# Mamba-2 scan and low-rank mixer on one core: V loaded in four transfers, begun behind B and C of the second pair

## The chip, the cores and the metric

The kernel runs on one NeuronCore of one Trainium2 chip. The time is device microseconds (us) of one execution of the program; smaller is better. Several runs of the kernel before are given, and one further execution was recorded by the hardware profiler.

## The reference: a chunked scan, then a mixer

The inputs are x (4 batches, 8 heads, 768 steps, 32 wide), a decay a per step, and B and C (16 wide). The scan, cut to what matters:

```python
for c in range(nc):                       # chunks of 32 steps
    cum = np.cumsum(la, axis=-1)          # la = log of the clipped decays
    L = np.exp(cum[:, :, :, None] - cum[:, :, None, :]) * causal
    M = (Cc @ Bc.T) * L
    y[:, :, sl] = M @ xc + (Cc @ state) * np.exp(cum)[..., None]
    state = decay_full * state + sum_j(Bc[j] xc[j] * decay_from_j[j])
```

Its output, with the heads joined to 256 channels, goes through the mixer:

```python
h = xt @ U @ V                            # over the 768 steps, rank 32
u = x + h.transpose(0, 2, 1)
out = u + np.maximum(u @ w_ch1, 0.0) @ w_ch2
```

U (768 x 32), V (32 x 768) and both weights w_ch1 (256 x 1024) and w_ch2 (1024 x 256) are handed over in double precision.

## The kernel before

**Tiling.** A batch's 768 steps are six blocks of 128, one step per partition. Two blocks make a pair, and the twelve pairs (three a batch) are numbered through. B and C of a pair lie in a tile `bc`, x in a tile `x`.

**Loads.** All loads are issued by SyncE (SP), by `begin` (L195 and L196). The B of one pair is two transfers, one a block, with C of the pair issued between them (`load_bc`, L200); x is two transfers (`load_x`, L213). The doubles arrive as pairs of 32-bit words in tiles called `words`. U and V share one of these: `load_v` (L254) fills its second half, `load_u` (L258) its first. V is 32 rows of 768 doubles, cut into four pieces of 192 columns; piece q goes to the partitions from 32q to 32q + 31, so that a partition gets 384 words, or 1536 bytes. Before, one transfer does this: its source pattern has the piece q outermost (4), then 32 rows, then 384 words; its destination has 128 partitions.

**Order.** The order of work is written out by hand. `PLANS[0]` (L35) lists the first loads, which SP issues in that order behind the load of a (L182): B0 is B and C of pair 0, X0 its x, U0 and V0 are U and V. `PLANS[1]` to `PLANS[4]` list the steps of the other engines and the later loads; `follow` (L974) reads them. Lags are counted in pairs against the batch, so that in `PLANS[1]` the index -3 is pair 0 and -2 is pair 1.

**The first steps.** `F5` and `F4` put idle products on TensorE (PE) ahead of the next step. `A0` and `A1` (`decays`, L357) make the decay factors F of all pairs from a, by PE and ScalarE (ACT). `Q` (`prep`, L461) multiplies a part of B or C with F on VectorE (DVE) into the tile `BC`; Q-3.2, Q-3.1 and Q-3.0 are C and the two B of pair 0. `V-3.0.0` and `V-3.1.1` (`turn`, L511; these words have nothing to do with the matrix V) transpose them on PE into T and Cm. `Q-2.0` is B of pair 1, block 0; it stands on DVE ahead of the Cm of V-3.1.1. `K0` (`keep`, L376) makes the factors FD and `kept` by five groups of products on PE, then by `own` and `kept` on DVE (L394 to L397). Q-2.2 and Q-2.1 are C and the other B of pair 1.

`c0` is the first conversion step of U and V together (`to_fp32`, L401): two operations on DVE (L415, L417) and one on ACT (L419), which wait for both. Then come `D` (B times FD into `bd`, L473, on GpSimd in the first batch), `g` (products of T and Cm), `m` and `M` (masks on DVE), `s` and `u` (states), and `n`, `i` and `j` (products into y). `v0` (`spread`, L927) and the mixer use the finished V about twenty microseconds later.

DVE and GpSimd operations of one engine run in program order; DVE's operations all carry line 170, where a helper records them.

Of the kernel before, what the change touches and what calls it, by code (L numbers as in the profile page):

```python
# [32 lines left out]

PLANS = {
    0: (  # L35
        'V0 B0 X0 B1 U0 X1 B2 X2 B3 '),
    1: (
        'F5 A0 A1 Q-3.2 Q-3.1 Q-3.0 F4 V-3.0.0 Q-2.0 V-3.1.1 K0 Q-2.2 Q-2.1 c0 D-3 g-3 D-2 s-3 '
        'V-2.0.2 m-3 u-3 F2 V-2.1.2 M-3 E-1.1 Q-1.0 n-3 c0 g-2 i-3 Q-1.2 E-1.0 Q-1.1 w0 m-2 s-2 '
# [37 lines left out]
def kernel(  # L77
# [31 lines left out]
    NC = S // P  # L109
    NPR = NC // 2  # L110
    DM = NH * D
    RK = moe_U.shape[1]
# [7 lines left out]
    Q = 32  # L120
# [38 lines left out]
    class Kept:  # L159
# [6 lines left out]
        def __getattr__(self, name):  # L166
# [16 lines left out]
        out=a_sb,  # L183
        in_=a.rearrange("(g b) h (c s) -> g (b h c) s", g=2, s=P).rearrange(
            "g r s -> r g s"))
# [4 lines left out]
    def hold(load, until):  # L190

        tc.add_manual_dep(load.ins, until.ins.name, mybir.DependencyInfo(
            mybir.DependencyClass.Sync, mybir.DependencyReason.DATA))

    def begin(**kwargs):  # L195
        op = nc.sync.dma_start(**kwargs)  # L196
        if until:
            hold(op, until.pop())
# [24 lines left out]
    UV = const.tile([P, 2, NC * RK], FP32)  # L223
# [9 lines left out]
    def words_of(dst):  # L233
        p, i, j = dst.shape
        t = raw.tile([P, 2 * WCOLS], INT32, tag="words", name="words", bufs=NWORDS)
        weights.append((dst, t[:p, :2 * i * j]))
        return t[:p, :2 * i * j]
# [10 lines left out]
    U2, V2, w12, w22 = (w.bitcast(INT32) for w in (moe_U, moe_V, moe_w_ch1, moe_w_ch2))  # L248
# [3 lines left out]
    own = {}  # L252

    def load_v():  # L254
        own["UV"] = words_of(UV)
        begin(out=own["UV"][:, 2 * NC * RK:], in_=V2.rearrange("r (q j) -> q r j", q=4))

    def load_u():  # L258
        begin(out=own["UV"][:, :2 * NC * RK].rearrange("p (c r) -> p c r", c=NC),
# [24 lines left out]
    for word in PLANS[0].split():  # L284
        dict(loads, V=lambda n: load_v(), U=lambda n: load_u())[word[0]](int(word[1:]))
# [42 lines left out]
    for g in range(2):  # L328
# [3 lines left out]
        out=la.rearrange("p b c h -> p b h c"),  # L332
# [128 lines left out]
    def prep(k, c=0, n=2):  # L461

        b, q = pairs[k]
        if "BC" not in st.setdefault(k, {}):
            st[k]["BC"] = att.tile([P, 2, 2, NH, N], FP32, tag="BC", name="BC")
        for g in [slice(4) if n == 2 else slice(c, c + 1) if c < 2 else slice(2, 4)]:
            part = st[k]["BC"].rearrange("p i c h n -> p (i c) h n")[:, g]
            vector.tensor_tensor(
                out=part, in0=bc_sb[k].rearrange("p h i c n -> p (i c) h n")[:, g],
                in1=F[:, b, q].rearrange("p h i c -> p (i c) h")[:, g, :, None].to_broadcast(  # L470
                    part.shape), op=ALU.mult)
# [490 lines left out]
    def ytokens_of(k, v):  # L962
# [4 lines left out]
                 j=crossed, y=yout, t=ytokens, L=load, Q=lambda k, c: prep(k, c, 1),  # L967
# [59 lines left out]
```

## Time and profile before

| | |
|---|---|
| Runs of the kernel before | 227.67, 228.96 and 229.0 us, median 228.96 |
| Profiled execution, whole | 229.59 us |
| Its span, first to last instruction | 227.0 us |
| Mean granted TensorE clock | 0.985 |
| Busy: PE, PEld | 218.4 us (96%), 182.2 us (80%) |
| Busy: DVE, ACT, GpSimd | 158.1, 120.9, 6.4 us |
| Chain that ended last | PE 90%, DVE 4%, SP's queue 3%, DMA 1% |
| The load of V | issued at 1.26 us, 192 KB |
| The load of U | issued at 9.32 us, 192 KB, 3.1 us from issue to landing |

The profile divides the span into 40 slices and gives busy tenths of each engine:

```profile
PE   7779999999999999999999999999999999999994
PEclk9995999999999999999999999999999999999999
DMA  3997868990970021662005300200000010010011
```

PE is busy throughout but for the first slices of 5.7 us each. `PEclk` is the clock that PE was granted. The chain of waits is read from the end of the kernel back to its start: every step is the work, the issue or the transfer that released the next one.

### The profile page before, as it was taken

The page shows a single profiled execution, that of the slowest core. Times are in us where ns is not written, and L with a number is a line of the kernel's source. Part 1 is how long each engine was busy: PE and PEld are TensorE (multiplying, and loading weights), DVE is VectorE, ACT ScalarE, POOL GpSimd, SP SyncE. Part 2 cuts the span into 40 slices and gives each one's busy share as a digit, 9 for nine tenths or more (in the row PEclk, how much of TensorE's full clock was granted, in tenths as well). Part 3 has the DMA queues.
Part 4 walks back from the last instruction along what each step waited for, and adds up shares of the span by engine and source line. Part 5 has one row for each costly group of instructions (what it writes and reads, how often), then busy time and mean ns, then how long its engine had stood idle before and what let it go on. Part 6 is the DMA issues. An engine that isn't in the chain of part 4 may idle for free.

```text
span 227.0 us, 6988 instructions
## 1 busy us (share of the span) xinstructions
PE 218.4 (96%) x3016; PEld 182.2 (80%) x3016; DVE 158.1 (70%) x339; ACT 120.9 (53%) x283; POOL 6.4 (3%) x22
## 2 busy tenths in 40 slices
PE   7779999999999999999999999999999999999994
PEld 5648866665675768868998998799998799999994
DVE  3396999897998685879628827878566925765641
ACT  2263565778885334944635715386355524834820
POOL 4032000000000000000000000000000000000000
PEclk9995999999999999999999999999999999999999
DMA  3997868990970021662005300200000010010011
GB/s 79 138 126 119 99 166 222 230 220 8 184 98 1 3 72 15 86 86 72 4 0 75 90 2 3 75 0 0 4 0 3 23 49 0 1 69 3 0 69 69
DMA packets 69234, 14.56 MB, mean 64 GB/s; under 512 B 63508, under 2 KB 67412, under 8 KB 69204
## 3 DMA queue, kind: packets, MB, share of 16 engines
q1 hardware_dynamic: 69204, 14.13, 31.7%
q8 instruction: 23, 0.38, 0.7%
q14 instruction: 7, 0.06, 0.1%
HBM read 10.98 MB, written 3.15 MB: 62 GB/s over the span
## 4 chain that ended last, share of the span: by engine, by line
PE 90%; DVE 4%; SPq 3%; DMA 1%; issue 1%; DVEq 0%
PE x L773 33%; PE z L773 31%; PE y L677 4%; PE y L653 4%; PE w L727 3%; SPq L196 2%; PE w L900 2%; PE x L527 2%; PE w L698 2%; PE w L562 2%; PE w L495 2%; PE x L738 1%; DMA bc<-in_B_dram 1%; PE z L527 1%; DVE BC L170 1%; PE z L738 1%
## 5 line engine op out<-in xcount | busy, mean ns | idle before, releaser
L170 DVE SCALAR_TENSOR_TENSOR words<-words 128x768 fp32r<-128x768 f32 (+6 forms) x44 | 34.6, 804 | 2.1 <-ACT words L419 1.1
L773 PE MATMUL z<-u,w 128*128 128x384 f32 x144 | 32.9, 349 | 0.0
L773 PE MATMUL x<-u,w 128*128 128x384 f32 x144 | 32.6, 346 | 0.0
L778 ACT ACTIVATE x<-x 128x384 f32<-128x384 f32 (+1 forms) x31 | 14.6, 470 | 28.0 <-PE x L773 27.4
L773 PEld LDWEIGHTS z<-u,w 128*128 128x128 f32 x144 | 24.9, 188 | 1.4 <-ACT z L778 0.2
L773 PEld LDWEIGHTS x<-u,w 128*128 128x128 f32 x144 | 24.9, 188 | 1.0
L773 PE MATMUL x<-words,w 128*128 128x384 f32 x120 | 24.7, 340 | 0.2 <-DVE yT L170 0.2
L773 PE MATMUL z<-words,w 128*128 128x384 f32 x120 | 24.6, 336 | 0.0
L778 ACT ACTIVATE z<-z 128x384 f32<-128x384 f32 (+1 forms) x30 | 14.2, 473 | 14.7 <-PE z L773 14.3
L170 DVE SCALAR_TENSOR_TENSOR words<-x,words 128x384 fp32r<-128x384 f32 x24 | 13.3, 553 | 11.7 <-ACT words L807 11.7
L773 PEld LDWEIGHTS x<-words,w 128*128 128x128 f32 x120 | 20.8, 188 | 0.6 <-DVE yT L170 0.4
L773 PEld LDWEIGHTS z<-words,w 128*128 128x128 f32 x120 | 21.1, 188 | 0.0
L170 DVE TENSOR_TENSOR yT<-x,yT 128x384 f32<-128x384 f32 x15 | 8.3, 555 | 16.0 <-PE x L773 15.4
L170 DVE SCALAR_TENSOR_TENSOR words<-z,words 128x384 fp32r<-128x384 f32 x24 | 13.2, 552 | 4.9 <-ACT words L807 4.9
L807 ACT ACTIVATE words<-x 128x384 fp32r<-128x384 f32 x24 | 11.8, 491 | 6.7 <-PE x L773 6.5
L807 ACT ACTIVATE words<-z 128x384 fp32r<-128x384 f32 x24 | 11.8, 491 | 4.5 <-PE z L773 4.5
L170 DVE TENSOR_TENSOR yT<-z,yT 128x384 f32<-128x384 f32 x15 | 8.3, 553 | 8.3 <-PE z L773 8.3
L170 DVE TENSOR_TENSOR BC<-bc,F 128x512 f32<-128x512 f32 (+2 forms) x18 | 9.6, 553 | 4.7 <-ACT F L372 2.5
L170 DVE SCALAR_TENSOR_TENSOR S<-S,kept,w 128x64 f32<-128x64 f32 x40 | 11.2, 280 | 2.2 <-issue 0.5
L653 PEld LDWEIGHTS y<-T,Sm 32*64 32x64 f32 x352 | 9.0, 136 | 4.5 <-issue 1.4
L653 PE MATMUL y<-T,Sm 32*64 32x64 f32 x352 | 12.3, 243 | 0.3 <-DVE settled L170 0.3
L677 PEld LDWEIGHTS y<-M,x 64*32 64x32 f32 x768 | 9.1, 110 | 3.4 <-issue 1.7
(139 smaller groups left out, 387.5 us busy)
## 6 DMA issues: line engine op xcount, KB each, us to landing
words<-in_moe_w_ch_dram SPq DMA_DIRECT2D x7, 512.0 KB, 4.3
x<-in_x_dram SPq DMA_DIRECT2D x24, 128.0 KB, 3.4
out_dram<-o SPq DMA_DIRECT2D x5, 384.0 KB, 2.5
bc<-in_B_dram SPq DMA_DIRECT2D x24, 64.0 KB, 3.3
bc<-in_C_dram SPq DMA_DIRECT2D x12, 128.0 KB, 3.0
out_dram<-words SPq DMA_DIRECT2D x2, 384.0 KB, 4.0
words<-in_moe_w_ch_dram SPq DMA_DIRECT2D x2, 256.0 KB, 3.4
out_dram<-o SPq DMA_DIRECT2D x3, 128.0 KB, 1.7
```

Source lines behind the costliest of these rows:

```text
L170: self.last = call(*args, **kwargs)
L196: op = nc.sync.dma_start(**kwargs)
L495: nc.tensor.transpose(out=tp[:, i, v], in_=s["BC"][:, i, c + v].rearrange("p h n -> p (h n)"), identity=ident)
L527: nc.tensor.matmul(out=g[r][cols, c], lhsT=s["T"][rows, 0, c, cols], rhs=s["Cm"][rows, :, :, ts(2 * c + p, Q)].rearrange("r v t i -> r v i ...
L562: nc.tensor.matmul(out=s["A"][p][ts(r, Q), v], lhsT=s["bd"][half, v, 2 * r:2 * r + 2].rearrange("p h n -> p (h n)"), rhs=x_sb[k][half, v, ...
L653: product = nc.tensor.matmul(out=y[p][ts(r % 2, H), r // 2, c], lhsT=own[ts(r, Q)], rhs=s["T"][ts(r, Q), 1, :, ts(2 * c + p, Q)].rearrange ...
L677: product = nc.tensor.matmul(out=y[p][ts(i, Q), n, c], lhsT=x_sb[k][half, c, h], rhs=s["M"][half, h // 2, c, h % 2], start=fresh(k, p, [i] ...
L698: nc.tensor.transpose(out=t[:, c, g], in_=yT[b][:, g, ts(2 * q + c, P)], identity=ident)
L727: nc.tensor.matmul(out=p[ts(q, Q)], lhsT=U_sb[:, c], rhs=ytok[b][:, c, ts(q // 2, P)], start=(c == 0), stop=(c == NC - 1), skip_group_chec ...
L773: nc.tensor.matmul(out=t, lhsT=lhsT, rhs=rhs, start=start, stop=True, skip_group_check=True)
L778: nc.scalar.activation(t, t, AF.Copy, scale=1.0 + EPS)
L807: nc.scalar.activation(gs[j, m // 2][0][:, m % 2], t, AF.Relu, scale=NEAR)
```

## The change

V is loaded by four transfers, one for each piece, instead of one, each from a plain block of 32 rows and 384 words to 32 partitions. And they are issued behind B and C of pair 1 and ahead of U, instead of first.

```diff
 PLANS = {
     0: (
-        'V0 B0 X0 B1 U0 X1 B2 X2 B3 '),
+        'B0 X0 B1 V0 U0 X1 B2 X2 B3 '),
...
     def load_v():
         own["UV"] = words_of(UV)
-        begin(out=own["UV"][:, 2 * NC * RK:], in_=V2.rearrange("r (q j) -> q r j", q=4))
+        for q in range(4):
+            begin(out=own["UV"][ts(q, Q), 2 * NC * RK:], in_=V2[:, ts(q, 2 * NC * RK)])
```

`ts(q, n)` is the slice from q n to (q + 1) n; Q is 32 and 2 * NC * RK is 384. The place of V's tile among the `words` tiles moves with it, and so does the SP queue: a, B, C, B, x, x (pair 0), B, C, B (pair 1), four parts of V, U, x, x (pair 1), then the loads of pair 2. The order of instructions on PE, DVE, ACT and GpSimd is the same in both kernels.

## Prediction

> **What bounds the kernel now.** I read the engine table first: PE is busy 218.4 of 227.0 us, so whatever PE waits for early on is paid at the end. The slices show that the only weak PE digits stand in the first 15 us, beside a DMA digit that is low (3) in the very first slice. So I went to the chain of waits, in order of time (start, length, who):
> ```profile
> 1.26 0.71 SPq L196
> ...
> 3.13 2.69 SPq L196
> ...
> 7.12 3.19 DMA bc<-in_B_dram
> ...
> 10.33 0.03 DVE BC L170
> ...
> 10.54 0.60 DVE Cm L170 x2
> 11.14 0.44 DVE own L170
> ...
> 11.61 0.52 DVE kept L170
> 12.13 1.32 DVE BC L170 x2
> 13.45 0.54 DVE words L170 x2
> 13.99 0.34 DVE M L170
> ```
> The end of the kernel hangs on SP's issues up to 7.1, then on the landing of one B (pair 1, block 0) at 10.31, then on DVE until 16.2, and from there on PE. The 2.69 us is one DMA issue (the second B of pair 0) where its neighbours take 0.43 to 0.71. The timeline of DVE says what the late B costs:
> ```profile
> 7.36 0.83 DVE L170 TENSOR_TENSOR BC<-bc,F 128x256 f32<-128x256 f32 x3 [2.52 <-ACT F L372]
> 10.33 0.29 DVE L170 TENSOR_TENSOR BC<-bc,F 128x128 f32<-128x128 f32 x1 [2.14 <-DMA bc<-in_B_dram]
> 12.04 1.41 DVE L170 TENSOR_TENSOR BC<-bc,F 128x256 f32<-128x256 f32 x2
> ```
> DVE stands idle 2.14 us for it, and its first BC waited for F, not for data. Stretch by stretch (length, PE, PEld, DVE, ACT, POOL busy, clock, DMA share, GB/s) the transfers are far from full until 7 us:
> ```profile
> 3.00:4.00 1.00, 1.00 (x7) 1.00 (x6) 0.54 (x2) 0.03 (x1) 0.25 (x2) 1.00 0.40 88
> 5.00:6.00 1.00, 1.00 (x6) 1.00 (x6) 0.00 (x0) 0.00 (x0) 0.00 (x0) 1.00 0.51 75
> 7.00:8.00 1.00, 1.00 (x4) 0.54 (x4) 0.64 (x3) 0.33 (x1) 0.00 (x0) 1.00 1.06 154
> ```
> Why: the trace's semaphore records have V's last four increments at 6.14, 6.19, 6.22 and 6.25, where other loads have sixteen, and the 128 packets of V (1536 B, 65 ns each when undisturbed) run from 2.5 to 5.5. B and C of pair 0, issued behind V, land in twelve parts by 5.45 and 6.03 and in four parts at 6.37 to 6.48 and 6.79 to 6.91. So V sits on four DMA engines, the loads behind it wait there, and the fifth issue sticks until V is through (5.82).
>
> **What the Trainium skill says.** "DMA: Bandwidth & Descriptors", "Why a DMA increments its semaphore by 16 and not by 1": a transfer runs on the largest count up to 16 that divides the slowest dimension of both patterns. Before, V has 128 and 4 (q outermost), so four; a transfer of the change has 32 and 32, so sixteen. The four increments agree. The same page, "Rules for kernel authors", advises one 128-partition transfer rather than parts, since parts share the same 16 engines; the trace of before shows a whole that does not have sixteen. "SBUF — State Buffer", "SBUF: two separate sides": a VectorE operation with two SBUF inputs and a GpSimd one lock each other out. Agrees: the two BC beside bd (POOL, 11.93 to 13.30) took 0.78 and 0.71 us, the same shapes elsewhere 0.43 and 0.29. "TensorE: Matmul & The Clock Gate", Part 1: after an idle window of about 3.4 us, free-running, the clock is halved. Agrees: the clock is 0.5 from 16.33 to 23.16, twice 3.41.
>
> **The change, part by part.**
> *V leaves the front.* One issue of 0.71 plus 0.06 goes: B, C and B of pair 0 are issued 0.77 earlier. The sticking issue should take an ordinary 0.58 in place of 2.69. From a's end at 1.20, with 0.43 for the first B and about 0.62 each after it, the B of pair 1 is issued at 4.2 rather than 7.12, 2.9 earlier.
> *What the transfers allow.* Packet records at full flow give 450 B packets (64 B) or 380 x or C packets (128 B) per quarter us, so 0.55 us for a B (1024) and 0.68 for x or C. First B packets came 1.5 after their issue: 2.8 here. B, C, B, x, x, B then is 3 x 0.55 + 3 x 0.68 = 3.7: data through at 6.5, landed about 7.0 against 10.31. Were half of that lost, 8.6. DVE wants it at 8.19 (7.36 + 0.83), so its 2.14 wait goes, or 0.4 of it stays.
> *What is late next.* Not F: the fills on PE hold it at 7.33 as before. After the early BC (8.19 to 8.48) comes Cm, whose transposes end on PE at 8.91: 8.95 to 9.55. Then "own" waits for K0's products, on PE until 10.37 and behind nothing that moves: 10.40 instead of 11.06, a gain of **0.66**. This wait takes the place of the one removed.
> *Behind it.* own 0.52 and kept 0.52 end at 11.44. FD on ACT stood behind T, and T behind Cm: from 11.51 to about 9.9, so bd on POOL starts about 10.2 rather than 11.93 and is through at 11.6. own reads PSUM, kept has one input, so by the page neither should be locked out, and the two BC start at 11.42 with bd nearly done: 0.43 + 0.29 less overlap = 0.65 rather than 1.41, another **0.7**. No row shows own or kept beside POOL; if they were held as BC was, the 0.7 is lost, not more. I take 0.65: **1.3** in all, DVE's words at 12.1 instead of 13.38.
> *Four V issues ahead of U.* Each is 32 rows, 2 packets per engine; the nearest rows are a (0.40) and a weight load of 256 rows (0.37). No row has 32 rows: 0.37 below, 0.79 (the dearest ordinary issue) above; I take 0.42, plus 0.04 between, 1.8 in all. Data cost 128 x 65 ns / 16 = 0.5 us. B of pair 1, block 1, is issued by 6.6 instead of 9.27, so V by 8.4 and U by 9.0 (before 9.90), landing about 10.9 against 12.41. Queued behind V on SP: U, both x of pair 1, the loads of pair 2. x lands near 11.5 and 12.2 (13.31 and 14.32), pair 2's last B near 14 (17.04), wanted about 15.8. No other queue is passed; ACT's and POOL's orders stay. The new waits on five semaphores rather than two ahead of words (DVE at L415, ACT at L419) I put at 0 to 0.2, covered on ACT by its idle time.
> *After 12 us.* DVE's words, M, S, M are back to back until 16.2 and move as one; PE's first product on the second pair's path (y, 16.24) and all after it move by the same 1.3. No wait on a DMA ends a PE stall after 17 us, so nothing there gives it back; the weights' issues wait mostly on DVE and move with it.
> *Sum.* 229.59 of the profiled execution (span 227.0, 2.6 around it) less 1.3 is 228.3. The median is 0.63 lower, 228.96: less 1.3 gives **227.7**.
>
> **The rivals.**
> *The clock is spared too (0.18).* The halved stretch follows the PE gaps at 10.4 to 11.3 and 12.9 to 14.4; the first goes. If the gate then stays open, products of 16.3 to 23.2 shrink: w transposes 0.63 for four at full clock against about 1.05, the others 0.1 to 0.5 a group, some 2.8 together, of which DVE, 70% busy there, lets through 1.5 to 2. Time 227.7 - 1.8 = 225.9. Against: the second gap, set by DVE, stays, and the windows are free-running, so it can fall either way in each run; 227.67 among the runs before may be such a one.
> *The gain is absorbed (0.12).* K0 or bd holds DVE as now, or the gap moves the clock's halving on to dearer products. For it: own moves by 0.66 only, and POOL's overlap is unseen. Time 228.4 to 229.0.
> *U too late: slower (0.08).* The stuck issue is not V's doing and stays, so only 0.77 is won ahead of U, while four V issues at 0.79 cost 3.2: U lands at 12.41 - 0.77 + 3.2 = 14.8. DVE wants it at 12.8 to 13.4; words, and behind it M, S and PE's next products, stand until 14.8, 1.4 later than now: 230.4. It decides from U landing after 13.4. Against: sticking ends as V's data ends, and of the loads behind V only four parts in sixteen are late. Here belongs the case that the parts do not run on sixteen.
>
> **How the numbers follow.** My forecast has 0.62 (own range 227.3 to 228.4 plus run noise, 0.7). The range takes in most of the spared clock below and the absorbed gain above: 225.8 to 229.3. About 1% (2.3 us) is what a measurement can tell from no change, and 1.3 is less. Faster by over 1%: the spared clock and a thin tail of the forecast, 0.22. Slower by over 1% needs 231.3, beyond the late U: 0.04. Within: 0.74.
>
> **What would show it.** V has 16 increments per part and no SP issue before 5 us takes over 1 us; DMA share at 3 to 6 us is over 0.8; the B of pair 1 lands by 8.2; DVE's wait for it is gone, and one of about 0.8 for K0's z stands before own; bd starts near 10.2 and the two BC behind kept take 0.65; words start near 12.1 and y near 14.9. It is wrong if words waits for U or V, if own or kept stretch beside bd, or if the issue still sticks.

## The result, and the profile after

| | before | after |
|---|---|---|
| Median | 228.98 us (20 runs, 227.67 to 230.15) | 227.58 us (20 runs, 226.89 to 228.99) |
| Profiled execution, its span | 229.59, 227.0 us | 226.89, 225.2 us |
| First M on DVE (behind words) | 13.91 us | 12.85 us |
| Second group of y on PE | 16.24 us | 15.17 us |
| First M of pair 2 on DVE | 18.38 us | 16.74 us |

The ratio of the times is 0.9947, 95% interval 0.9927 to 0.9967: a gain of about 1.2 us, between 0.8 and 1.7 (the medians alone differ by 1.4). The forecast was 227.7. All ratios here leave out runs over 1.5% above the fastest of the same kernel, so that a range of times told with the last experiments is wider than its ratio. The two profiled executions differ by more than the kernels do, 2.7 us: that of before is 0.6 above its median, that of after is the fastest of its 20.

The chain of waits of the kernel after, in order of time (start, length, who), shows SP's issues and what hangs on them:

```profile
3.10 0.69 SPq L196
...
4.78 0.58 SPq L196
...
7.68 0.42 SPq L196
...
9.07 0.42 SPq L196
...
10.75 1.19 SPq L196
11.94 0.04 issue
11.98 4.13 DMA bc<-in_C_dram
16.11 0.02 issue
16.14 0.68 DVE BC L170 x2
```

The issue of 2.69 us is gone: nothing before 5 us takes more than 0.90. B of pair 1 is issued at 4.78 (7.12 before), a part of V in 0.42 (the first in 0.67), U at 9.07. The chain no longer passes through B of pair 1. It now stays on SP and DMA until 16.1, where C of **pair 2** lands: a new bound. The semaphore records have 16 increments for each part of V, one for each DMA engine that had a share of it (four before, for the whole), and B of pair 1 landing at 7.68 instead of 10.31.

Stretch by stretch (length, PE, PEld, DVE, ACT, POOL busy, clock, DMA share, GB/s) the transfers from 3 to 6 us are fuller than the 0.40 and 0.51 of before, and from 7 us about as full as its 1.06:

```profile
3.00:4.00 1.00, 1.00 (x7) 1.00 (x7) 0.49 (x1) 0.00 (x0) 0.27 (x2) 1.00 0.90 126
5.00:6.00 1.00, 1.00 (x7) 1.00 (x6) 0.00 (x0) 0.00 (x0) 0.00 (x0) 1.00 0.92 145
7.00:8.00 1.00, 1.00 (x12) 0.79 (x8) 0.27 (x1) 0.45 (x2) 0.00 (x0) 1.00 1.01 140
```

The timeline of DVE after (start, busy, instructions, the idle time before them and who ended it):

```profile
7.74 1.03 DVE L170 TENSOR_TENSOR BC<-bc,F 128x256 f32<-128x256 f32 x4 [2.81 <-ACT F L373]
9.31 0.61 DVE L170 TENSOR_SCALAR Cm<-w,slot 128x128 f32<-128x128 f32 x2 [0.55 <-PE w L496]
10.78 0.53 DVE L170 TENSOR_TENSOR own<-z,mine 128x352 f32<-128x352 f32 x1 [0.86 <-PE z L391]
11.34 0.52 DVE L170 TENSOR_REDUCE kept<-own 128x44 f32<-128x352 f32 x1
11.78 0.62 DVE L170 TENSOR_TENSOR BC<-bc,F 128x256 f32<-128x256 f32 x2
12.31 0.62 DVE L170 TENSOR_SCALAR words<-words 128x384 int32<-128x384 int32 x2
12.85 0.74 DVE L170 TENSOR_TENSOR M<-x,causal 128x256 int32<-128x256 int32 x2
...
15.71 1.11 DVE L170 TENSOR_TENSOR BC<-bc,F 128x128 f32<-128x128 f32 x3 [0.26 <-DMA bc<-in_B_dram]
```

The fourth BC (B of pair 1) now follows the first three without a gap. The 2.14 us wait is replaced by 0.55 for the transposes ahead of Cm (w) and 0.86 for K0's products (z). The two BC behind kept take 0.62, not 1.41. Each of these is a step of the forecast.

### The profile page after: what moved, and what is told of

The parts are those of the page before. It is cut to its first block, busy times and chain, and to the rows that moved or that the text cites. A ratio compares the mean times of both kernels' runs of the same rounds, so it can differ in the third digit from the quotient of the medians.

```text
span 225.2 us, 6994 instructions
## 1 busy us (share of the span) xinstructions
PE 217.0 (96%) x3016; PEld 180.5 (80%) x3016; DVE 157.3 (70%) x339; ACT 120.8 (54%) x283; POOL 6.2 (3%) x22
## 4 chain that ended last, share of the span: by engine, by line
PE 89%; SPq 5%; DVE 2%; DMA 2%; issue 1%
PE x L774 33%; PE z L774 31%; SPq L196 4%; PE y L678 4%; PE y L654 4%; PE w L728 3%; PE w L901 2%; PE w L699 2%; PE x L528 2%; DMA bc<-in_C_dram 2%; PE w L496 2%; PE w L563 2%; PE x L739 2%; PE z L528 1%; PE z L739 1%
## 5 line engine op out<-in xcount | busy, mean ns | idle before, releaser
L678 PE MATMUL y<-M,x 64*32 64x64 f32 x768 | 11.3, 224 | 1.0 <-issue 0.7
```

Source lines behind the costliest of these rows:

```text
L678: product = nc.tensor.matmul(out=y[p][ts(i, Q), n, c], lhsT=x_sb[k][half, c, h], rhs=s["M"][half, h // 2, c, h % 2], start=fresh(k, p, [i] ...
```

## Where the time came from

F, and with it the first BC on DVE, opened the row at 7.74 rather than 7.36. PE begins each execution with a stretch of slow products, and this stretch ended later here, as the timeline of PE shows for the same two groups, first before,

```profile
5.80 0.64 PE L365 MATMUL w<-la,ref 128*128 128x192 f32 x2
6.37 0.56 PE L369 MATMUL w<-la,ref 128*64 128x96 f32 x8
```

then after:

```profile
5.88 0.85 PE L366 MATMUL w<-la,ref 128*128 128x192 f32 x2
6.65 0.64 PE L370 MATMUL w<-la,ref 128*64 128x96 f32 x8
```

The same products took 0.85 and 0.64 instead of 0.64 and 0.56, with no wait between them. (The trace's clock records begin at 6.09 us before and at 6.88 after. Ahead of its first record a stretch shows a clock of 1.00 for want of one.) The change touches neither group; the experiments below have F anywhere from 6.76 to 8.04. So I count from F: to the first M it was 13.91 - 7.36 = 6.55 us before and is 12.85 - 7.74 = 5.11 after, 1.44 less (forecast 1.3). Of this, F to own went from 3.70 to 3.04 (0.66, as worked out), and own to words from 2.32 to 1.53 (0.79; 0.65 was taken).

The granted clock also differs: 13 of the 20 runs after were near full clock (0.9975 or more), while of the 181 runs of the kernel before that the experiments are compared with only 54 were. (The clocks of the 20 runs before are not on record.) How much is that worth? Core spans by clock:

| granted clock | before | after |
|---|---|---|
| 0.9975 and over | 226.45 us (54 runs) | 225.6 us (13) |
| 0.99 to 0.9945 | 227.2 us (79) | none |
| 0.97 to 0.987 | 227.7 us (48) | 226.2 us (7) |

At equal clock the gain is 0.85 to 1.5 us. A fit of the span against the time under a halved clock (twice the clock's shortfall times the span; on average 3.8 us a run before, 2.6 after) gives 0.14 us for each such microsecond before and 0.10 after. The difference of 1.2 us is thus worth some 0.15 us of the gain, by this estimate. The rest, about 1 us, agrees with the shorter path.

## Experiments: shape or place

The change does two things to V's load. Each was done alone, and the clog was made worse. Clog is short for what the kernel before shows: V's data goes over four DMA engines alone, and the loads behind it wait there.

**The shape alone.** Four parts, where V stood before. Diff against the kernel after:

```diff
-        'B0 X0 B1 V0 U0 X1 B2 X2 B3 '),
+        'V0 B0 X0 B1 U0 X1 B2 X2 B3 '),
```

> V in four parts, but first of all (shape alone). Theory, four DMA engines clogged by V's shape: sixteen increments per part, no SP issue over 1 us before 6 us; the V issues push B of pair 1 about 1.9 later than in the change, landing near 9.5, which still hides behind K0's products (own at 10.4 to 10.8): 227.6, ratio 0.994. Rival, the place at the front does it: B of pair 1 lands after 10, DVE's wait for it stays near 2 us, 229.0, ratio 1.000.

Measured: 228.70 us, ratio 0.9976 (0.9951 to 1.0002), less than half of the gain expected and by itself not clear of no gain at all. The clog is gone (16 increments a part, all landed by 4.49), but B of pair 1 lands at 9.78, so the timeline of DVE for this kernel reads:

```profile
9.80 0.29 DVE L170 TENSOR_TENSOR BC<-bc,F 128x128 f32<-128x128 f32 x1 [1.29 <-DMA bc<-in_B_dram]
10.01 0.60 DVE L170 TENSOR_SCALAR Cm<-w,slot 128x128 f32<-128x128 f32 x2
10.73 0.53 DVE L170 TENSOR_TENSOR own<-z,mine 128x352 f32<-128x352 f32 x1
...
11.73 1.19 DVE L170 TENSOR_TENSOR BC<-bc,F 128x256 f32<-128x256 f32 x2
```

own starts as early as after the whole change (10.73 against 10.78), since K0 hides the later B. What it loses stands below: the two BC take 1.19, not 0.62. Cm ran at 10.01 rather than 9.31, so T, FD and bd came later. The timeline of POOL has bd at 11.39 here,

```profile
11.39 1.38 POOL L479 TENSOR_TENSOR bd<-bc,FD 128x256 f32<-128x256 f32 x2 [8.07 <-DMA words<-in_moe_U_dram]
```

and after the whole change at 10.70:

```profile
10.70 1.20 POOL L479 TENSOR_TENSOR bd<-bc,FD 128x256 f32<-128x256 f32 x2 [7.37 <-ACT FD L385]
```

A bd that runs to 12.77 covers the BC pair; one that ends at 11.90 nearly misses it. The expected size had taken a pair that misses bd. (The releaser named on the first line, U, landed only at 12.31, after bd had begun: an inferred releaser that the times contradict.)

**The lock-out alone.** The kernel after, with the first bd held until own is written, and nothing else:

```diff
-        vector.tensor_tensor(
+        keeping["own"] = vector.tensor_tensor(
...
-        (vector if b else nc.gpsimd).tensor_tensor(
+        done = (vector if b else nc.gpsimd).tensor_tensor(
...
+        if k == 0:
+            hold(done, keeping["own"])
```

> The change, with the first bd on GpSimd held until own is written, so that it runs beside the two BC again. Theory, that half of the gain is the end of this lock-out: the two BC take about 1.3 instead of 0.62 and words start near 13.0 instead of 12.3; of the 0.7 the wait for pair 2's B and C (0.3 to 0.5 in the trace of the change) hides a part: 227.9 to 228.3, ratio to before 0.995 to 0.997. Rival, the lock-out costs nothing on the path: 227.6, ratio 0.994.

Measured: 228.06 us, ratio 0.9972 (0.9951 to 0.9992), the time as expected. From its timeline of DVE:

```profile
10.80 1.20 DVE L170 TENSOR_TENSOR BC<-bc,F 128x256 f32<-128x256 f32 x2
12.68 0.63 DVE L170 TENSOR_SCALAR words<-words 128x384 int32<-128x384 int32 x2 [0.68 <-DMA words<-in_moe_U_dram]
```

Holding bd makes the pair take 1.20 again. The second line shows a further limit: F was early in this execution (6.76), and words then waited for U, landed at 12.55, so that in this one execution the slower pair cost words nothing. The two kernels lose 0.0025 to 0.0029, or about 0.6 us, of the change's gain, and that is also what the BC pair lost. But the intervals of the three ratios overlap: that the pair slows beside bd is shown by the traces; that this is the half of the gain is only consistent with them.

**The place alone.** V as one transfer, where the change puts it. Diff against the kernel before:

```diff
-        'V0 B0 X0 B1 U0 X1 B2 X2 B3 '),
+        'B0 X0 B1 V0 U0 X1 B2 X2 B3 '),
```

> V whole, but behind B and C of pair 1 (place alone). Theory: V again has four increments, but what it clogs is U, x of pair 1 and the loads of pair 2; B of pair 1 lands near 7.7 and own starts at 10.4 to 10.8; words waits for U until about 12.4, so 0.1 to 0.5 of the gain is lost at most: 227.6 to 228.2, ratio 0.994 to 0.997. Rival, the shape does it wherever V stands: pair 2's loads come late and words stands, 229.0 or more, ratio 1.000.

Measured: 229.42 us, ratio 1.0017 (0.9995 to 1.0038). The gain I expected did not come; the rival's outcome held. The queue of SP (start, length, what was issued) and, below it, DVE:

```profile
8.47 2.87 SPq L196 DMA_DIRECT2D x<-in_x_dram  x2
11.38 2.02 SPq L196 DMA_DIRECT2D bc<-in_B_dram  x1
13.45 1.05 SPq L196 DMA_DIRECT2D bc<-in_C_dram  x1
```

```profile
12.08 0.62 DVE L170 TENSOR_TENSOR BC<-bc,F 128x256 f32<-128x256 f32 x2
13.76 0.63 DVE L170 TENSOR_SCALAR words<-words 128x384 int32<-128x384 int32 x2 [1.06 <-DMA words<-in_moe_U_dram]
```

Up to the BC pair it is the kernel after (B of pair 1 landed at 8.05, the pair took 0.62). But the clog has moved with V: its four increments come at 12.73 to 13.26, U has twelve parts by 12.11 and the last four at 13.41 to 13.66, and the issues behind stick for 2.29 us (the second x of the first line) and 2.02. words waits 1.06 for U, and the gain is spent. The intervals of this kernel and of the change do not meet: at the new place, the shape is what the gain needs.

**More clog.** The kernel before, V in two transfers of 64 partitions, each with its piece (2) outermost:

```diff
-        begin(out=own["UV"][:, 2 * NC * RK:], in_=V2.rearrange("r (q j) -> q r j", q=4))
+        for h in range(2):
+            begin(out=own["UV"][ts(h, H), 2 * NC * RK:],
+                  in_=V2[:, ts(h, 4 * NC * RK)].rearrange("r (q j) -> q r j", q=2))
```

> V first, in two transfers of 64 partitions with the piece outermost (2), so twice the packets on half the engines. Theory: two increments each, both on the same two engines, 64 packets x 65 ns = 4.2 us there; the sticking issue lasts until about 8, B of pair 1 lands near 12, U near 13.7: 230.0 to 230.5, ratio 1.004 to 1.007. Rival, only V's bytes at the front count: as before, 229.0.

Measured: 231.3 us, ratio 1.0112 (1.0079 to 1.0146); the direction was right, the size nearly double. Two increments each (5.96 and 6.21, 8.00 and 8.28), and SP's queue:

```profile
3.96 4.08 SPq L196 DMA_DIRECT2D bc<-in_B_dram  x1
8.09 1.23 SPq L196 DMA_DIRECT2D x<-in_x_dram  x2
```

One issue sticks for 4.08 us, until 8.04, as V's second half is ending. The whole front moves: even the first BC waits for data, not for F (it starts at 9.24). The rule in the Trainium skill, "DMA: Bandwidth & Descriptors", "Why a DMA increments its semaphore by 16 and not by 1", gives two, four and sixteen for the three shapes, and the counts agree. Ordered by it, with V first each time, the ratios are 1.0112, 1 and 0.9976 (the last with an interval up to 1.0002).

## Experiments: what bounds the kernel now

These take one limit of the kernel after away at a time. Diffs are against it, but for the first.

**Fewer idle products ahead of F**, in the kernel before and in the kernel after:

```diff
-        'F5 A0 A1 Q-3.2 Q-3.1 Q-3.0 F4 V-3.0.0 Q-2.0 V-3.1.1 K0 Q-2.2 Q-2.1 c0 D-3 g-3 D-2 s-3 '
+        'F2 A0 A1 Q-3.2 Q-3.1 Q-3.0 F4 V-3.0.0 Q-2.0 V-3.1.1 K0 Q-2.2 Q-2.1 c0 D-3 g-3 D-2 s-3 '
```

> The kernel before, with two idle products ahead of the decays instead of five, so F is ready about 1.3 earlier. Theory, the late B of pair 1 (10.3) hides F before the change: DVE's wait for F shrinks, its wait for B grows by as much, 229.0, ratio 1.000. Rival, F is on the path of both kernels: 227.9, ratio 0.995.

> The change with two idle products instead of five. Theory, after the change F and K0 hold the path until own, but U, landing at 12.0 to 12.5, stands just behind it: own comes 1.0 to 1.3 earlier, words waits for U and starts at 12.0 to 12.5 as in the change: 227.4 to 227.7, ratio 0.993 to 0.995. Rival, F and K0 alone hold it: words near 11.2, 226.5, ratio 0.989.

Measured: before 229.00, ratio 0.9987 (0.9967 to 1.0006), nothing: B of pair 1 lands at 10.43 whatever F does, and even the first BC, at 7.26, comes hardly earlier in its trace (7.36 before), since C of pair 0 lands only at 7.17. After 228.09, ratio 0.9954 (0.9937 to 0.9971), no better than the change itself and just short of what was expected. Its timeline of DVE:

```profile
9.50 0.53 DVE L170 TENSOR_TENSOR own<-z,mine 128x352 f32<-128x352 f32 x1 [0.76 <-PE z L391]
...
12.75 0.63 DVE L170 TENSOR_SCALAR words<-words 128x384 int32<-128x384 int32 x2 [1.55 <-DMA words<-in_moe_U_dram]
...
17.98 0.29 DVE L170 TENSOR_TENSOR BC<-bc,F 128x128 f32<-128x128 f32 x1 [0.98 <-DMA bc<-in_B_dram]
```

own is 1.28 earlier, words 0.44 later: U lands at 12.63. That is the forecast's late-U rival at its true size: a limit on any further gain, not a loss.

**Conversion later**: the first c0 moved from ahead of D-3 to ahead of Q-1.0, so that M does not stand behind U.

```diff
-        'F5 A0 A1 Q-3.2 Q-3.1 Q-3.0 F4 V-3.0.0 Q-2.0 V-3.1.1 K0 Q-2.2 Q-2.1 c0 D-3 g-3 D-2 s-3 '
-        'V-2.0.2 m-3 u-3 F2 V-2.1.2 M-3 E-1.1 Q-1.0 n-3 c0 g-2 i-3 Q-1.2 E-1.0 Q-1.1 w0 m-2 s-2 '
+        'F5 A0 A1 Q-3.2 Q-3.1 Q-3.0 F4 V-3.0.0 Q-2.0 V-3.1.1 K0 Q-2.2 Q-2.1 D-3 g-3 D-2 s-3 '
+        'V-2.0.2 m-3 u-3 F2 V-2.1.2 M-3 E-1.1 c0 Q-1.0 n-3 c0 g-2 i-3 Q-1.2 E-1.0 Q-1.1 w0 m-2 s-2 '
```

> The change with the first conversion step of U and V put ten steps later, behind the state and the second mask of pair 0, so that nothing on DVE's path waits for U. Theory: M starts at 12.3 instead of 12.85 and no run waits for U; pair 2's B and C, landing at 16.1 to 16.5, take back most of it: 227.2 to 227.5, ratio 0.992 to 0.994. Rival, U is the only thing behind the gain's end: 226.8 or less, ratio 0.991.

Measured: 227.94, ratio 0.9960 (0.9937 to 0.9983); the gain expected did not come. The first M stands at 11.59, 1.26 earlier than after the change; F was 0.72 early in this execution (7.02), so that 0.54 is due to the order. Then, on DVE:

```profile
15.51 0.29 DVE L170 TENSOR_TENSOR BC<-bc,F 128x128 f32<-128x128 f32 x1 [0.78 <-DMA bc<-in_B_dram]
16.12 0.43 DVE L170 TENSOR_TENSOR BC<-bc,F 128x256 f32<-128x256 f32 x1 [0.31 <-DMA bc<-in_C_dram]
17.86 0.29 DVE L170 TENSOR_TENSOR BC<-bc,F 128x128 f32<-128x128 f32 x1 [1.32 <-DMA bc<-in_B_dram]
```

All is given back to B and C of pair 2, 2.4 us of waits in this execution.

**B and C of pair 2 ahead of x of pair 1**:

```diff
-        'B0 X0 B1 V0 U0 X1 B2 X2 B3 '),
+        'B0 X0 B1 V0 U0 B2 X1 X2 B3 '),
```

> The change with one move only: the loads of pair 2's B and C go ahead of x of pair 1. Theory, the landing of pair 2's B and C (16.1 to 17.8 in the traces behind the change) takes back part of the gain: they land by about 14.5, DVE's wait for them goes, words still waits for U: 227.0 to 227.4, ratio 0.991 to 0.994. Rival, x of pair 1, now landing at 15.5 to 17, becomes the wait: 227.8 or more, ratio 0.995 or above.

Measured: 228.02, ratio 0.9965 (0.9944 to 0.9987); a miss, with the rival's number. DVE no longer waits for pair 2 (its BC at 15.64 for 1.03). The rival's cause is not shown, though: x of pair 1 lands at 16.14 and 16.61, but no wait for it stands in the trace. words waits 0.19 for U, PE stands 1.06 for the first M behind it (0.78 after the change), and at 20.3 us it stands 0.71 (0.44) for something that the profile doesn't name. What took the gain stays open.

**Both**: B2 ahead of V, and the two lines of the late conversion as above; and the same with F2 in place of F5:

```diff
-        'B0 X0 B1 V0 U0 X1 B2 X2 B3 '),
+        'B0 X0 B1 B2 V0 U0 X1 X2 B3 '),
```

> As the run with the late conversion, and the loads of pair 2's B and C go ahead of V and U, x of pair 1 stays behind these. Theory, three waits in a row end the gain (K0, U, pair 2's landing), and this takes away the last two: pair 2's B lands by 12.5, DVE's wait there goes, 226.5 to 227.0, ratio 0.989 to 0.992. Rival, pair 2's landing isn't on the path: as the late conversion alone, 227.2 to 227.5.

> The run with late conversion and pair 2 ahead of V and U, with two idle products instead of five. Theory, with U and pair 2 off the path F and K0 hold it, so what was worth nothing in the change is worth something here: own about 1 us earlier, y of pair 0 near 14; of it at most the wait for B of pair 1 is lost: 226.3 to 227.0, ratio 0.987 to 0.990. Rival, the idle products keep the clock up and are worth more than F: the clock is halved for longer, 227.6 or more, ratio 0.993.

Measured: 227.6 (7 runs), ratio 0.9926 (0.9898 to 0.9954), and 227.36 (13 runs), ratio 0.9927 (0.9904 to 0.9950). The first fell just short of its expectation, the second clearly. With F2 the first M is at 11.05, the earliest but for nothing: DVE, then PE in the same kernel:

```profile
15.34 0.63 DVE L170 TENSOR_SCALAR words<-words 128x384 int32<-128x384 int32 x2 [1.69 <-DMA words<-in_moe_U_dram]
```

```profile
16.07 0.77 PE L563 MATMUL w<-x,bd 64*32 64x64 f32 x32 [0.91 <-DMA x<-in_x_dram]
```

In the kernel after, the late conversion, the new order and these two, the last of pair 2's B and C and pair 1's x lands at 16.5 to 17.8 us. In three of the five DVE or PE waits for one of these loads, up to 0.26, 1.32 and 0.91 us; in the new order and the first of these two no such wait stands in the trace.

**U and V last of all**, the first c0 ahead of j-2 and the second behind y-2; and the same with F2:

```diff
-        'B0 X0 B1 V0 U0 X1 B2 X2 B3 '),
+        'B0 X0 B1 B2 X1 X2 B3 V0 U0 '),
...
-        'j-3 y-3 u-2 V-1.0.2 M-2 F1 V-1.1.3 F1 s-1 n-2 B4 u-1 i-2 g-1 j-2 P0 B5 y-2 T0 T0 O-3.0 '
+        'j-3 y-3 u-2 V-1.0.2 M-2 F1 V-1.1.3 F1 s-1 n-2 B4 u-1 i-2 g-1 c0 j-2 P0 B5 y-2 c0 T0 T0 O-3.0 '
```

The two c0 of the lines ahead of this one are taken out.

> The change with V (four parts) and U behind all loads of pairs 2 and 3, and their first two conversion steps moved behind the state of pair 2. Theory, in the change U and V stand in the stream of loads ahead of what the scan needs and hold DVE at words; with both out of the way only F and K0 hold pair 0 and no wait for a load is left on DVE until 20 us: M at 12.2 to 12.6, 226.3 to 227.0, ratio 0.988 to 0.992. Rival, the four V issues and U only move the wait to the later weights: 227.6 or more, ratio 0.994.

> As the run with U and V last, with two idle products instead of five ahead of the decays. Theory, with no load in the way the earlier F is at last worth its time: M at about 11.1, 225.5 to 226.5, ratio 0.984 to 0.989. Rival, the transfers of x and of pair 2 and 3 hold DVE and PE whatever stands ahead: no better than the run with five idle products.

Measured: ratio 0.9994 (0.9970 to 1.0018) and 0.9977 (0.9944 to 1.0010); both missed. The medians of all their 22 runs, 229.38 and 229.98 us, even lie above the 228.86 of the kernel before. The front is at last free (first M of pair 2 at 15.43 in the second, the earliest of all), and the wait returns later, on DVE and behind it on PE:

```profile
21.23 0.63 DVE L170 TENSOR_SCALAR words<-words 128x384 int32<-128x384 int32 x2 [1.78 <-DMA words<-in_moe_U_dram]
```

```profile
21.98 0.50 PE L654 MATMUL y<-T,Sm 32*64 32x64 f32 x16 [1.34 <-DVE settled L170]
```

U's landing was only moved to 21 us, with "settled" and the states queued behind words on DVE. The times of the second kernel follow the granted clock from 226.7 to 227.4 us at 1.0 (5 runs) up to 229.8 to 231.2 at 0.983 to 0.985 (9 runs), more than the change itself does between its two clocks (0.6 us). A fit as above, over all 22 runs, gives 0.45 and 0.46 us for each microsecond under the halved clock in these two kernels, over three times the 0.10 to 0.14 of the change and of before; why the same shortfall costs more here was not tried.

No variant beats the change by more than the intervals hold: the best, 0.9926 and 0.9927, have intervals that contain its 0.9947.

## Why the prediction was right

- **Clog gone by the shape: right.** 16 increments a part, no sticking issue before 5 us, DMA shares of 0.90 and 0.92 where 0.8 was asked. The whole at the new place (1.0017) shows that the shape is needed.
- **B of pair 1: right, somewhat late.** Landed 7.68 against 7.0 (8.6 if half was lost), inside the 8.2 asked. Its issue at 4.78 was 0.6 later than worked out, because three issues took 0.69 to 0.90 where 0.62 was taken, and the gaps of 0.04 between them were not counted.
- **K0 takes the wait's place: right to the hundredth**, 3.04 us from F to own.
- **The lock-out ends: right.** bd at 10.70 (10.2 plus the 0.38 of the late F, and 0.1), the BC pair 0.62 (0.65). own and kept, whose overlap with POOL no row showed, took 0.53 and 0.52 beside bd: they are not held, as the Trainium skill, "SBUF — State Buffer", "SBUF: two separate sides", says of operations without two SBUF inputs.
- **V's issues: right in size**, 0.42 each but for the first (0.67). The issue of U ended at 9.49, where 9.0 was worked out: the loads ahead of V were already 0.33 late.
- **Data behind V: mis-sized.** U landed 2.90 after its issue, at 11.97, where 10.9 was forecast; x of pair 1 at 13.05 and 13.96 (11.5 and 12.2), the last B of pair 2 at 16.50 (14). For U the working took 1.9 from the end of its issue to its landing; before the change this was 2.51, and after it 2.48. The engines were not empty then: their mean share from 10 to 14 us is 0.98. words had 0.34 left to U. Pair 2, wanted "about 15.8", was late, and "nothing there gives it back" was wrong by 0.26 us of wait on DVE. Most of pair 2 was in time: fifteen of sixteen parts of its first B had landed by 14.27 and of its C by 14.98; one part of each came at 15.68 and 16.11 (see the last section).
- **The sum: right for partly other reasons.** 1.44 counted from F, less 0.26 at pair 2, with about 0.15 for the clock, is about 1.3 by this rough estimate; 1.2 (0.8 to 1.7) was measured. That the median of 227.58 lies 0.12 from the forecast is luck: the interval of the gain alone is 0.9 wide.
- **The clock rival: half right.** The halved stretch is gone from the profiled execution and rarer in the runs, but it is worth 0.10 to 0.14 us per halved microsecond: 0.7 to 1.0 for the 6.83 us stretch of before, where 1.5 to 2 were priced. Why so little reaches the end was not tried. Of the idle window that the prediction names, the trace bears out only the length: in the 3.41 us ahead of the halved stretch (12.92 to 16.33) PE was busy for 1.90.
- **Late U: not met, but near.** It binds as soon as F comes early (words waits 0.68 in the kernel with bd held, 1.55 with F2).

## What to carry to other kernels

Read the semaphore increments of each early load: a transfer that has four where its neighbours have sixteen held up the loads issued behind it at both places tried, and splitting it paid although each part costs an issue. The advice of the Trainium skill, "DMA: Bandwidth & Descriptors", "Rules for kernel authors", to prefer one 128-partition transfer has wholes in mind that run on all sixteen engines; it did not hold for one that runs on four (at the same place 1.0017 against 0.9947), a case that the same section has in its row "Use all 16 engines". When a wait is removed, ask which engine now runs beside which (the slower BC beside bd is about the size of half the gain here), and price the loads further down the queue as the next bound, not as slack.

## What the runs showed of the hardware that was not expected

- **An issue stuck until the data that lagged was nearly through.** 2.69 us in the kernel before (to 5.82; V's last increment 6.25), 4.08 with the halves (to 8.04; 8.28), and 2.29 and then 2.02 with the whole behind (to 13.40; 13.26). V is not needed for it: in the kernel after, an issue of x takes 1.95 from 13.30, to 15.25, while one part in sixteen of pair 2's first B is missing until 15.68.
- **Late parts of loads coincide with instruction fetches.** The queue table of the kernel after has 23 packets in the instruction queue, 0.38 MB, or 16 KB each:

```profile
q8 instruction: 23, 0.38, 0.7%
```

  0.7% of sixteen engines' 225.2 us is 25 us, 1.1 us a packet. One begins at 13.62 in the kernel after and takes 0.92; of the three loads under way then (pair 2) fifteen parts had landed by 14.27, 14.98 and 15.43, and the last part at 15.68, 16.11 and 16.50. In the kernel with F2 and both orders one begins at 12.62, and the last of V's 64 parts comes at 14.73, 1.71 behind its neighbours. That the fetch is the cause is not shown: the times coincide, and an execution without such fetches was not made.
- **The first slow stretch of PE shifts the whole front.** F came between 6.76 and 8.04 us in kernels with the same idle products ahead of it, so single executions can't be compared at a few tenths unless counted from F. It follows the time of the first clock record in all nine such traces: 4.76 us and F at 6.76, 6.09 and 7.36, 6.88 and 7.74, 7.65 and 8.04. In the first of these, with bd held, one idle product takes 0.42 us before that time and 0.275 after it.
